# A spectral mixer and a token MLP, forward and backward: one table loaded in two parts, four normal forms on another engine, a first load in two halves, three evictions on another engine

## The chip, the cores and the metric

The kernel runs on one core of one Trainium2 chip. The metric is the device time of one execution in microseconds (us). The core has TensorE (PE, matmuls; its weight loads are PEld), VectorE (DVE), ScalarE (ACT), GpSimd (POOL) and SyncE (SP), which issues most of the DMA transfers. Each engine works through its own instructions in a fixed order and waits on semaphores.

## The reference, cut to what matters

The reference is a forward pass of two blocks and all its gradients but that of B_x:

```python
x = A_x                                   # 1 x 2048 x 448
h  = x + irfft2(rfft2(layernorm(x)) * (w_r + 1j * w_i))
n  = layernorm(layernorm(h))              # one inside block B, one ahead of it
u  = gelu(einsum("bsd,sf->bdf", n, w1) + b1)             # F = 1792
h2 = h + transpose(einsum("bdf,fs->bds", u, w2) + b2)
# and the gradients of h2 for x, w_r, w_i, w1, b1, w2, b2, given grad_out
```

There are eight outputs: h2 and seven gradients. The gradient of w2 (out_6, 1792 x 2048) is gelu's output times grad_out; that of w1 (out_4, 2048 x 1792) is the normalized h times the gradient at gelu's input.

## The kernel before, in words

**Layout.** The 2048 rows are held as 128 partitions of 16 rows each (row 16q + h lies in partition q at place h), so that x, its normal form xln and so on are tiles of 128 x 16 x 448. A group is four of the 16 places.

**Front.** `Norm.stats` takes mean and variance of each place on VectorE (L278, L280). After four places `Norm.finish` (L284) takes the square root on ScalarE, the reciprocal and two small products on VectorE, and then writes the four normal forms. Each is one instruction, either a tensor_scalar on VectorE (L297) or an ACTIVATE on ScalarE (L300); the condition in L296 chooses. `fft_rows` (L304) folds a group into even and odd parts `eo` (L307 to L309, VectorE) and multiplies them by a small table (L315); the four results are evicted into `zt` (L316, through the helper `ev`, whose lines are L194 for ScalarE and L195 for VectorE). All this is run for four groups (L430).

`fft_cols` (L319) then does the column transform: for r = 0, 8 and 1 to 7 it multiplies parts of zt by the table df1 (L333 to L347), evicts (L339 or L350), forms sum and difference on VectorE (`gg`, L353), and calls `out_r` for r and 16 - r, three matmuls with the table `hf` (L325 to L327) and an eviction into xs (L328). hf has three planes: cosines, sines, and the negated sines, which VectorE writes (L462, through `neg`, L198). The first two are loaded by one transfer of 1 MB (L449). `cmul` (L359) multiplies by the spectral weights on VectorE, `ifft_cols` and `ifft_rows` go back. The same functions are run again for the gradient, with the same hf, on zt2 and ds (from L674).

**Loads.** `nxt` (L180) puts each early load behind the one before on SP's queue: x's group 0, half of grad_out (go_nat), x's group 1, the other half of go_nat, the first transposed block of w2 (w2T), x's groups 2 and 3, w2T's next four blocks, the tables df1 and hf, the two halves of w_t, three more blocks of w2T, the other tables. A w2T block needs one of four ring buffers, which `dg` frees.

**Matmuls that fill.** `dg(j)` (L438) needs w2T block j: 16 matmuls of 128 x 448 into one ps_mm buffer, evicted by ScalarE. dg(1) to dg(3) may be issued only after the row transforms of groups 0 to 2, dg(4) and later ones after that of group 3 (L440). `gw2(j)` (L661) computes one block of out_6 as four tiles of 128 x 512, each of four matmuls into a ps_mm buffer and one eviction; the string `on` says by tile which engine evicts. gw2(0) comes ahead of the last row transform, blocks 1 to 13 are written last in the program (L701) with "aaav": ScalarE three times, VectorE once. There are three ps_mm buffers and five ps_sp buffers; the transforms use the latter.

**Order.** The kernel's text isn't the order of the instructions. A planner takes the instruction that is ready and comes first in the text, by prices of its own, engine by engine, before the program is run; that is why dg's and gw2's matmuls lie between those of the transforms. `tc.issue_after(i)` forces what stands under it behind i on i's engine. In the run the order is fixed: an engine waits at an instruction that isn't ready, though later ones may be.

Of the kernel before, what the change touches and what calls it, by code (L numbers as in the profile page):

```python
# [11 lines left out]
BF16 = mybir.dt.bfloat16  # L12
# [5 lines left out]
P = 128  # L18
S = 2048
D = 448  # L20
DF = 225
# [3 lines left out]
NR = 16  # L25
# [4 lines left out]

def _bf(a):
    return np.ascontiguousarray(a.astype(ml_dtypes.bfloat16))


def _tables():

    tb = {}
    q = np.arange(P)
    t_q, pl_q = q // 8, q % 8
    same = (pl_q[:, None] == np.arange(8)[None, :]).astype(np.float64)
    kf = np.zeros((P, 16, 8))
    ke = np.zeros((16, 8, P))
    ko = np.zeros((16, 8, P))
    for r in range(9):
        al = 2 * np.pi * (t_q * r % 16) / 16
        kf[:, r, :] = np.cos(al)[:, None] * same  # L50
        if 0 < r < 8:
            kf[:, 16 - r, :] = -np.sin(al)[:, None] * same
        ke[r] = np.cos(al)[None, :] * same.T
        if 0 < r < 8:
            ke[16 - r] = -np.sin(al)[None, :] * same.T
            ko[16 - r] = -np.sin(al)[None, :] * same.T
        ko[r] = -np.cos(al)[None, :] * same.T
    tb["kf"] = _bf(kf.reshape(P, P))
    tb["kinv"] = _bf(np.stack([ke.reshape(P, P), ko.reshape(P, P), -ko.reshape(P, P)], 1))
    k2 = np.arange(DF)  # L60

    def dtab(scale):
        e = np.zeros((P, 2, DF))
        o = np.zeros((P, 2, 2, DF))
        de = np.stack([np.arange(P), np.arange(P) + 97], 1)
        do = np.stack([np.arange(P) + 1, np.arange(P) + 96], 1)
        for c in range(2):
            e[:, c] = np.cos(2 * np.pi * (de[:, c, None] * k2 % D) / D) * scale
            sn = np.sin(2 * np.pi * (do[:, c, None] * k2 % D) / D) * scale
            o[:, c, 0], o[:, c, 1] = -sn, sn  # L70
        e[: 128 - 97, 1] = 0
        o[: 129 - 96, 1] = 0
        return np.concatenate([e.reshape(P, -1), o.reshape(P, -1)], 1)

    wt = np.full(DF, 2.0 / (S * D))
    wt[[0, DF - 1]] = 1.0 / (S * D)
    tb["df1"] = _bf(dtab(wt))
    tb["df0"] = _bf(dtab(np.ones(DF)))

    def itab(w):  # L80
        a = np.zeros((P, 2, DF))
        b = np.zeros((P, 2, DF))
        d = np.arange(DF)
        for c in range(2):
            kk = np.arange(P) + 97 * c
            th = 2 * np.pi * (kk[:, None] * d[None, :] % D) / D
            a[:, c] = np.cos(th) * w[kk][:, None]
            b[:, c] = np.sin(th) * w[kk][:, None]
        a[: 128 - 97, 1] = 0
        b[: 128 - 97, 1] = 0  # L90
        return np.concatenate([a.reshape(P, -1), b.reshape(P, -1)], 1)

    tb["di0"] = _bf(itab(np.ones(DF)))

    wc = wt.copy()
    wc[0] = 0
    tb["di1"] = _bf(itab(wc))
    pp = np.arange(P)
    p = 16 * (pp % 8) + pp // 8
    r = np.arange(NR)  # L100
    th = 2 * np.pi * (p[:, None, None] * (16 * q[None, None, :] + r[None, :, None]) % S) / S
    tb["hf"] = _bf(np.stack([np.cos(th), np.sin(th)], 1))

    thi = th.transpose(2, 1, 0)
    hi = np.zeros((P, 2, NR, P))
    hi[:, 0, :9], hi[:, 1, :9] = np.cos(thi[:, :9]), np.sin(thi[:, :9])
    hi[:, 0, 9:], hi[:, 1, 9:] = -np.sin(thi[:, 9:]), -np.cos(thi[:, 9:])
    tb["hi"] = _bf(hi)
    tb["ident"] = _bf(np.eye(P))
    return tb  # L110
# [3 lines left out]
def kernel(  # L114
# [21 lines left out]
    ve, ac, po, pe = nc.vector, nc.scalar, nc.gpsimd, nc.tensor  # L136

    consts = ctx.enter_context(tc.tile_pool(name="consts", bufs=1))
# [41 lines left out]
    def nxt(load, *args):  # L180
        if chain:
            with tc.issue_after(chain[-1].ins):
                chain.append(load(*args))
        else:
            chain.append(load(*args))
# [11 lines left out]
    def neg(out, in_):  # L197
        ve.tensor_scalar(out=out, in0=in_, scalar1=-1.0, scalar2=None, op0=ALU.mult)  # L198

    def rows(ap):  # L200
        return ap.rearrange("(q h) d -> q h d", h=NT)


    x = slot(0, [P, NT, D], "x")

    def load_x(g):
        nxt(ld, x[:, 4 * g:4 * g + 4, :], rows(A_x[0])[:, 4 * g:4 * g + 4, :])

    load_x(0)
    tb = _tables()  # L210
    hnd = {k: nc.inline_tensor(v, name=f"tab_{k}") for k, v in tb.items()}
    eps_x = consts.tile([P, 1], F32, name="eps_x")
# [56 lines left out]
    class Norm:  # L269
# [14 lines left out]
        def finish(self, g):  # L284
            mv = self.mv[:, :].rearrange("p (i c) -> p i c", c=2)
            r = self.rstd[:, 4 * g:4 * g + 4]
            sq = col(4, f"sq_{self.nm}")
            ac.activation(out=sq[:], in_=mv[:, :, 1], func=ACT.Sqrt, bias=self.eps_col[:], scale=self.scale)
            ve.reciprocal(out=r, in_=sq[:])
            ve.tensor_scalar(out=self.rneg[:, 4 * g:4 * g + 4], in0=r, scalar1=self.back, scalar2=None, op0=ALU.mult)  # L290
            nb = col(4, f"nb_{self.nm}")
            ve.scalar_tensor_tensor(out=nb[:], in0=mv[:, :, 0], scalar=-1.0, in1=r, op0=ALU.mult, op1=ALU.mult)
            for i in range(4):
                h = 4 * g + i

                if i > 1 and (self.nm == "x" or g == 3):  # L296
                    ve.tensor_scalar(out=self.dst[:, h, :], in0=self.src[:, h, :], scalar1=self.rstd[:, h:h + 1],  # L297
                                     scalar2=nb[:, i:i + 1], op0=ALU.mult, op1=ALU.add)
                else:
                    ac.activation(out=self.dst[:, h, :], in_=self.src[:, h, :], func=ACT.Identity,  # L300
                                  scale=self.rstd[:, h:h + 1], bias=nb[:, i:i + 1])
# [14 lines left out]
            done = ev(zt[:, :, :, 8 * h:8 * h + 8], pz[:, :, :].rearrange("p c (s k) -> p c s k", k=8), on[i])  # L316
        return last, done

    def fft_cols(zt, dtab, dst):  # L319
        e_t = dtab[:, 0:2 * DF].rearrange("p (c k) -> p c k", c=2)  # L320
        o_t = dtab[:, 2 * DF:6 * DF].rearrange("p (c s k) -> p c s k", c=2, s=2)

        def out_r(r, gg):
            px = ps_sp([P, 2 * DF])
            pe.matmul(px[:, :], lhsT=hf[:, 0, r, :], rhs=gg[:, :], start=True, stop=False)  # L325
            pe.matmul(px[:, 0:DF], lhsT=hf[:, 1, r, :], rhs=gg[:, DF:2 * DF], start=False, stop=False)
            pe.matmul(px[:, DF:2 * DF], lhsT=hf[:, 2, r, :], rhs=gg[:, 0:DF], start=False, stop=True)  # L327
            ac.copy(out=dst[:, :, r * DF:(r + 1) * DF], in_=px[:, :].rearrange("p (c k) -> p c k", c=2))  # L328

        for r in (0, 8, 1, 2, 3, 4, 5, 6, 7):  # L330
            pr = ps_sp([P, 2 * DF])
            for c in range(2):
                pe.matmul(pr[:, 0:DF], lhsT=zt[:, c, r, :], rhs=e_t[:, c, :], start=(c == 0), stop=(c == 1))  # L333
            for c in range(2):
                pe.matmul(pr[:, DF:2 * DF], lhsT=zt[:, 2 + c, r, :], rhs=o_t[:, c, 0, :],
                          start=(c == 0), stop=(c == 1))
            if r in (0, 8):
                gg = k1([P, 2 * DF], "gg")
                ac.copy(out=gg[:], in_=pr[:])  # L339
                out_r(r, gg)  # L340
                continue
            pi = ps_sp([P, 2 * DF])
            for c in range(2):
                pe.matmul(pi[:, 0:DF], lhsT=zt[:, 2 + c, 16 - r, :], rhs=o_t[:, c, 1, :],
                          start=(c == 0), stop=(c == 1))
            for c in range(2):
                pe.matmul(pi[:, DF:2 * DF], lhsT=zt[:, c, 16 - r, :], rhs=e_t[:, c, :],  # L347
                          start=(c == 0), stop=(c == 1))
            gi = f2([P, 2 * DF], "gi")
            ac.copy(out=gi[:], in_=pi[:])  # L350
            for rr, op in ((r, ALU.add), (16 - r, ALU.subtract)):
                gg = k1([P, 2 * DF], "gg")
                ve.tensor_tensor(out=gg[:], in0=pr[:], in1=gi[:], op=op)  # L353
                out_r(rr, gg)


    R_GROUPS = ((0, 3), (14, 16), (3, 6), (11, 14), (6, 8), (8, 11))
# [70 lines left out]
    zt = slot(2, [P, 4, NR, P], "zt")  # L428
# [16 lines left out]

    dg(0)
    df1 = table([P, 6 * DF], "df1", "df")
    hf = consts.tile([P, 3, NR, P], BF16, name="hf")
    nxt(ld, hf[:, 0:2], hnd["hf"].ap())  # L449
    w_t = slot(4, [P, 2, XW], "w_t")  # L450
    load_w(w_t, nxt)
    for j in range(1, 4):
# [6 lines left out]
    for g in range(4):  # L459
        nxt(ld, xln_d[:, 4 * g:4 * g + 4, :], xln[:, 4 * g:4 * g + 4, :])  # L460
    with tc.issue_after(folded[3][1].ins):
        neg(hf[:, 2], hf[:, 1])  # L462
    xs = slot(3, [P, 2, XW], "xs")

    def neg_hi(r0, r1, last):
# [1 line left out]
            with tc.issue_after(last.ins):  # L467
                neg(hi[:, 0], hi[:, 2])

    fft_cols(zt, df1, xs)  # L470
    cmul(lambda r0, r1: (w_t[:, 0, r0 * DF:r1 * DF], w_t[:, 1, r0 * DF:r1 * DF]), xs, w_t, False, neg_hi)
    ab = slot(5, [P, 2, 2, NT, NR, 8], "ab")
    ifft_cols(w_t, ab)
# [225 lines left out]
    st(out_7.rearrange("(q h) -> q h", h=NT), gb2b[:])  # L699

    for j in range(1, NFB):  # L701
        s6_st = gw2(j, "aaav")
        if j == 8:
            s6_mid = s6_st

# [69 lines left out]
```

## Time and profile before

| what | us |
|---|---|
| runs: median (lowest to highest of 3) | 370.83 (369.65 to 373.05) |
| the profiled execution | 368.86 |
| its span | 367.1 |
| first matmul starts | 10.43 |
| matmuls, busy | 347.4 |
| VectorE, busy | 236.7 |
| ScalarE, busy | 213.8 |

The span runs from the first to the last instruction that the profile shows; the execution's time has a little more around it. Rows of the timeline are: start in us, length in us, engine, line of the kernel, operation, tile written <- tiles read, shapes, how many were merged into the row, and in brackets how long the engine stood idle ahead of it and what ended that wait. L169 and L175 are the helpers that issue loads and transposing loads, SPq is SP's queue of them: the length of its rows is the time to issue a transfer, not the time until the data is there.

### The profile page before, as it was taken

The numbers are of one execution on the slowest core, as the hardware profiler recorded it, in microseconds if no ns is written. First come the engines' busy times: TensorE is split into PE (matmuls) and PEld (weight loads), VectorE is DVE, ScalarE is ACT, GpSimd is POOL, SyncE is SP. The second block draws the span as 40 slices with busy tenths as digits, with TensorE's granted clock in tenths as the row PEclk, the third lists the DMA queues.
The fourth block names the chain that finished last, engine by engine and source line by source line (L and its number), as shares of the span: only waits on it lengthen the run. The fifth ranks groups of instructions, "written<-read, shape, count | busy, mean of one in ns | idle before, by whom it ended". The sixth has DMA issues, their size and how long they took to land.

```text
span 367.1 us, 5776 instructions
## 1 busy us (share of the span) xinstructions
PE 347.4 (95%) x2115; PEld 200.4 (55%) x2115; DVE 236.7 (64%) x562; ACT 213.8 (58%) x410; POOL 61.3 (17%) x107
## 2 busy tenths in 40 slices
PE   0898999999999999999999999999989999999996
PEld 0555666676655555555555555556655555565553
DVE  4863679887647999422267778378995666698000
ACT  3575554456649996029022245867656676787664
POOL 1000000001122112300630000101012531356211
PEclk9999999999999999999999999999999999999999
DMA  8999999996999999999989793992774444956533
GB/s 286 267 275 292 293 248 271 303 269 223 318 234 217 349 311 349 374 343 205 269 193 186 158 186 159 163 184 96 180 190 186 183 168 162 353 209 241 230 151 150
DMA packets 132524, 86.48 MB, mean 236 GB/s; under 512 B 91952, under 2 KB 123824, under 8 KB 131984
## 3 DMA queue, kind: packets, MB, share of 16 engines
q1 hardware_dynamic: 124304, 55.78, 61.5%
q0 software_dynamic: 8048, 30.31, 22.5%
q8 instruction: 16, 0.26, 0.3%
q14 instruction: 12, 0.10, 0.1%
q10 hardware_dynamic: 144, 0.03, 0.0%
HBM read 32.81 MB, written 30.76 MB: 173 GB/s over the span
## 4 chain that ended last, share of the span: by engine, by line
PE 64%; DVE 20%; ACT 9%; DMA 4%; issue 2%; ACTq 0%; DVEq 0%
PE ps_mm L736 12%; PE ps_mm L666 10%; PE ps_sp L591 7%; PE ps_mm L523 6%; PE ps_sp L523 5%; PE ps_mm L442 5%; PE ps_mm L591 4%; DMA w2T<-in_B_w_dram 3%; DVE junk L619 3%; DVE junk L621 3%; ACT v L614 3%; DVE t_r L366 2%; DVE gg L353 2%; PE ps_sp L415 2%; DVE t_i L367 2%
## 5 line engine op out<-in xcount | busy, mean ns | idle before, releaser
L194 ACT CAST s<-ps_mm 128x512 bf16<-128x512 f32 (+1 forms) x107 | 57.6, 557 | 25.6 <-PE ps_mm L666 11.1
L666 PE MATMUL ps_mm<-goT,g_t 128*128 128x512 bf16 x224 | 55.2, 379 | 1.6 <-ACT s L194 1.5
L442 PE MATMUL ps_mm<-go_nat,w2T 128*128 128x448 bf16 x224 | 50.3, 356 | 1.0 <-DMA w2T<-in_B_w_dram 1.0
L736 PE MATMUL ps_mm<-du_t,hlnT 128*128 128x512 bf16 (+1 forms) x256 | 49.6, 352 | 0.0
L647 PE MATMUL ps_mm<-du,w1T 128*128 128x449 bf16 x224 | 43.4, 353 | 0.0
L736 PEld LDWEIGHTS <-hlnT 128*128 128x128 bf16 x256 | 25.1, 98 | 22.2
L591 PE MATMUL ps_sp<-gT,w2c 128*128 128x448 bf16 x140 | 35.6, 352 | 0.0
L614 ACT ACTIVATE v<-ps_mm,nm,rstd_h 128x448 f32<-128x448 f32 x16 | 11.6, 724 | 40.2 <-DVE nm L612 40.2
L172 POOL DMA_DIRECT2D out_dram<-s x29 | 15.6, 539 | 114.0 <-ACT s L194 87.8
L591 PEld LDWEIGHTS <-w2c 128*128 128x128 bf16 x224 | 21.9, 98 | 20.5
L647 PEld LDWEIGHTS <-w1T 128*128 128x128 bf16 x224 | 21.7, 97 | 20.7
L666 PEld LDWEIGHTS <-g_t 128*128 128x128 bf16 x224 | 21.6, 97 | 20.7 <-issue 1.4
L523 PEld LDWEIGHTS <-w1c 128*128 128x128 bf16 x224 | 21.8, 98 | 20.1 <-issue 1.3
L442 PEld LDWEIGHTS <-w2T 128*128 128x128 bf16 x224 | 21.7, 98 | 16.1 <-DMA w2T<-in_B_w_dram 1.7
L353 DVE TENSOR_TENSOR gg<-ps_sp,gi 128x450 bf16<-128x450 f32 x28 | 16.2, 621 | 17.5 <-ACT gi L350 17.5
L591 PE MATMUL ps_mm<-gT,w2c 128*128 128x448 bf16 x84 | 25.0, 352 | 0.0
L523 PE MATMUL ps_mm<-hln,w1c 128*128 128x448 bf16 x112 | 23.8, 352 | 0.4 <-DVE b1col L512 0.2
L194 ACT CAST eo<-ps_sp 128x450 bf16<-128x450 f32 x32 | 17.2, 538 | 11.0 <-PE ps_sp L415 10.7
L596 DVE SCALAR_TENSOR_TENSOR h<-ps_sp,b2col,hr 128x448 bf16<-128x448 f32 x10 | 6.3, 679 | 25.7 <-PE ps_sp L591 25.7
L523 PE MATMUL ps_sp<-hln,w1c 128*128 128x448 bf16 x112 | 22.6, 352 | 0.0
L619 DVE CUSTOM_DVE_ANT_0 junk<-ps_sp,xr,rneg_x 128x448 bf16<-128x448 f32 x16 | 10.9, 682 | 16.3 <-ACT v L616 16.3
L315 PE MATMUL ps_sp<-kf,eo 128*128 128x128 bf16 x128 | 9.3, 231 | 11.9 <-DVE eo L309 11.9
(148 smaller groups left out, 622.0 us busy)
## 6 DMA issues: line engine op xcount, KB each, us to landing
w1c<-in_B_w_dram SPq DMA_DIRECT2D x7, 1024.0 KB, 8.4
w2c<-in_B_w_dram SPq DMA_DIRECT2D x8, 896.0 KB, 10.8
out_dram<-s POOLq DMA_DIRECT2D x14, 512.0 KB, 3.0
out_dram<-s POOLq DMA_DIRECT2D x15, 448.0 KB, 2.9
xs_d<-xs SPq DMA_DIRECT2D x1, 1800.0 KB, 7.7
xs_b<-xs_d SPq DMA_DIRECT2D x1, 1800.0 KB, 8.1
x<-in_A_x_dram SPq DMA_DIRECT2D x4, 448.0 KB, 4.2
go_nat<-in_grad_out_dram SPq DMA_DIRECT2D x2, 896.0 KB, 6.8
```

The source lines that it names most:

```text
L172: return (eng or po).dma_start(out=out, in_=in_)
L194: return ac.copy(out=out, in_=in_)
L353: ve.tensor_tensor(out=gg[:], in0=pr[:], in1=gi[:], op=op)
L442: pe.matmul(pg[:], lhsT=w2T[j][:, t, :], rhs=go_nat[:, t, :], start=(t == 0), stop=(t == NT - 1))
L523: pe.matmul(pu[:], lhsT=wc[:, h, o:o + P], rhs=hln[:, h, :], start=(h == 0), stop=(h == NT - 1))
L591: pe.matmul(p2[i][:], lhsT=w2c[t0 // 4][:, j, i * P:(i + 1) * P], rhs=gT[:, j, :], start=(j == 0), stop=(j == NFB - 1))
L614: ac.activation(out=v[:], in_=ps[:, 0:D], func=ACT.Identity, scale=rstd_c, bias=nm1[:])
L619: ve.tensor_tensor_reduce(out=junk[:], in0=ps[:, 0:D], in1=xhat, scale=rneg_c, scalar=0.0, op0=ALU.mult, op1=ALU.add, accum_out=nm2[:])
L621: ve.scalar_tensor_tensor(out=junk[:], in0=xhat, scalar=nm2[:], in1=v[:], op0=ALU.mult, op1=ALU.add)
L647: w1_last = pe.matmul(pd[:], lhsT=w1T[:, j, :], rhs=du[:, j, 0:D + 1], start=(j == 0), stop=(j == NFB - 1))
L666: mm = pe.matmul(pw[:], lhsT=g_t[:, c, j * P:(j + 1) * P], rhs=goT[:, c, 512 * n:512 * n + 512], start=(c == 0), stop=(c == 3))
L736: pe.matmul(pw[:, 0:wdt], lhsT=hlnT[:, c, h * P:(h + 1) * P], rhs=du_t[:, c, 512 * n:512 * n + wdt], start=(c == 0), stop=(c == 3))
```

## The change

There are four edits. The table hf is stored and loaded in two parts of eight r each, in the order R_ORDER in which out_r uses them (0, 8, 1, 15, 2, 14, 3, 13, then 4, 12 and so on); the first part is negated where the whole was, the second by a function that fft_cols calls after VectorE's sums for r = 2. In the second use of fft_cols the function isn't given, and the planes are those written in the first. x's group 0 is loaded in two transfers of two places each. The condition for normal forms now puts all four of x's group 3 on VectorE; x's other groups and h's are where they were. gw2's blocks 4, 5 and 6 are evicted by ScalarE alone.

```diff
+R_ORDER = [0, 8] + [k for r in range(1, 8) for k in (r, 16 - r)]
...
@@ -99,7 +102,8 @@
     p = 16 * (pp % 8) + pp // 8
     r = np.arange(NR)
     th = 2 * np.pi * (p[:, None, None] * (16 * q[None, None, :] + r[None, :, None]) % S) / S
-    tb["hf"] = _bf(np.stack([np.cos(th), np.sin(th)], 1))
+
+    tb["hf"] = _bf(np.stack([np.cos(th), np.sin(th)], 1)[:, :, R_ORDER].reshape(P, 2, 2, 8, P).transpose(0, 2, 1, 3, 4))
 
     thi = th.transpose(2, 1, 0)
     hi = np.zeros((P, 2, NR, P))
@@ -206,7 +210,8 @@
     def load_x(g):
         nxt(ld, x[:, 4 * g:4 * g + 4, :], rows(A_x[0])[:, 4 * g:4 * g + 4, :])
 
-    load_x(0)
+    for h in (0, 2):
+        nxt(ld, x[:, h:h + 2, :], rows(A_x[0])[:, h:h + 2, :])
     tb = _tables()
     hnd = {k: nc.inline_tensor(v, name=f"tab_{k}") for k, v in tb.items()}
     eps_x = consts.tile([P, 1], F32, name="eps_x")
@@ -293,7 +298,7 @@
             for i in range(4):
                 h = 4 * g + i
 
-                if i > 1 and (self.nm == "x" or g == 3):
+                if (i > 1 or g == 3) if self.nm == "x" else (i > 1 and g == 3):
                     ve.tensor_scalar(out=self.dst[:, h, :], in0=self.src[:, h, :], scalar1=self.rstd[:, h:h + 1],
                                      scalar2=nb[:, i:i + 1], op0=ALU.mult, op1=ALU.add)
                 else:
@@ -316,15 +321,16 @@
             done = ev(zt[:, :, :, 8 * h:8 * h + 8], pz[:, :, :].rearrange("p c (s k) -> p c s k", k=8), on[i])
         return last, done
 
-    def fft_cols(zt, dtab, dst):
+    def fft_cols(zt, dtab, dst, second=None):
         e_t = dtab[:, 0:2 * DF].rearrange("p (c k) -> p c k", c=2)
         o_t = dtab[:, 2 * DF:6 * DF].rearrange("p (c s k) -> p c s k", c=2, s=2)
 
         def out_r(r, gg):
             px = ps_sp([P, 2 * DF])
-            pe.matmul(px[:, :], lhsT=hf[:, 0, r, :], rhs=gg[:, :], start=True, stop=False)
-            pe.matmul(px[:, 0:DF], lhsT=hf[:, 1, r, :], rhs=gg[:, DF:2 * DF], start=False, stop=False)
-            pe.matmul(px[:, DF:2 * DF], lhsT=hf[:, 2, r, :], rhs=gg[:, 0:DF], start=False, stop=True)
+            k, i = R_ORDER.index(r) // 8, R_ORDER.index(r) % 8
+            pe.matmul(px[:, :], lhsT=hf[:, k, 0, i, :], rhs=gg[:, :], start=True, stop=False)
+            pe.matmul(px[:, 0:DF], lhsT=hf[:, k, 1, i, :], rhs=gg[:, DF:2 * DF], start=False, stop=False)
+            pe.matmul(px[:, DF:2 * DF], lhsT=hf[:, k, 2, i, :], rhs=gg[:, 0:DF], start=False, stop=True)
             ac.copy(out=dst[:, :, r * DF:(r + 1) * DF], in_=px[:, :].rearrange("p (c k) -> p c k", c=2))
 
         for r in (0, 8, 1, 2, 3, 4, 5, 6, 7):
@@ -350,8 +356,10 @@
             ac.copy(out=gi[:], in_=pi[:])
             for rr, op in ((r, ALU.add), (16 - r, ALU.subtract)):
                 gg = k1([P, 2 * DF], "gg")
-                ve.tensor_tensor(out=gg[:], in0=pr[:], in1=gi[:], op=op)
+                last = ve.tensor_tensor(out=gg[:], in0=pr[:], in1=gi[:], op=op)
                 out_r(rr, gg)
+            if r == 2 and second is not None:
+                second(last)
 
 
     R_GROUPS = ((0, 3), (14, 16), (3, 6), (11, 14), (6, 8), (8, 11))
@@ -445,8 +453,9 @@
 
     dg(0)
     df1 = table([P, 6 * DF], "df1", "df")
-    hf = consts.tile([P, 3, NR, P], BF16, name="hf")
-    nxt(ld, hf[:, 0:2], hnd["hf"].ap())
+    hf = consts.tile([P, 2, 3, 8, P], BF16, name="hf")
+    for k in range(2):
+        nxt(ld, hf[:, k, 0:2], hnd["hf"].ap()[:, k])
     w_t = slot(4, [P, 2, XW], "w_t")
     load_w(w_t, nxt)
     for j in range(1, 4):
@@ -459,7 +468,7 @@
     for g in range(4):
         nxt(ld, xln_d[:, 4 * g:4 * g + 4, :], xln[:, 4 * g:4 * g + 4, :])
     with tc.issue_after(folded[3][1].ins):
-        neg(hf[:, 2], hf[:, 1])
+        neg(hf[:, 0, 2], hf[:, 0, 1])
     xs = slot(3, [P, 2, XW], "xs")
 
     def neg_hi(r0, r1, last):
@@ -467,7 +476,12 @@
             with tc.issue_after(last.ins):
                 neg(hi[:, 0], hi[:, 2])
 
-    fft_cols(zt, df1, xs)
+
+    def neg_hf(last):
+        with tc.issue_after(last.ins):
+            neg(hf[:, 1, 2], hf[:, 1, 1])
+
+    fft_cols(zt, df1, xs, neg_hf)
     cmul(lambda r0, r1: (w_t[:, 0, r0 * DF:r1 * DF], w_t[:, 1, r0 * DF:r1 * DF]), xs, w_t, False, neg_hi)
     ab = slot(5, [P, 2, 2, NT, NR, 8], "ab")
     ifft_cols(w_t, ab)
@@ -699,7 +713,7 @@
     st(out_7.rearrange("(q h) -> q h", h=NT), gb2b[:])
 
     for j in range(1, NFB):
-        s6_st = gw2(j, "aaav")
+        s6_st = gw2(j, "aaaa" if 4 <= j <= 6 else "aaav")
         if j == 8:
             s6_mid = s6_st
```

## The prediction

> **What bounds the kernel now.** I read the busy table first, then TensorE's own rows in order of time, looking only for the spots where it stands, then the rows of the engine or queue named there as releaser.
>
> ```profile
> span 367.1 us, 5776 instructions
> PE 347.4 (95%) x2115; PEld 200.4 (55%) x2115; DVE 236.7 (64%) x562; ACT 213.8 (58%) x410; POOL 61.3 (17%) x107
> ```
>
> TensorE (PE) works 95% of the span. It starts at 10.43 us, and from there to its last matmul it hardly stands still, because low-priority matmuls (dg, then gelu_in, gw2, the last product) are put into every hole. A change can only win by an earlier useful start or by removing one of the few stands. These are the stands that this change can touch, and the row that causes each:
>
> ```profile
> 10.43 1.89 PE L315 MATMUL ps_sp<-kf,eo 128*128 128x128 bf16 x16 [10.43 <-DVE eo L309]
> 16.59 1.07 PE L315 MATMUL ps_sp<-kf,eo 128*128 128x128 bf16 x16 [0.55 <-DVE eo L309]
> 23.14 1.07 PE L315 MATMUL ps_sp<-kf,eo 128*128 128x128 bf16 x16 [0.38 <-DVE eo L309]
> 28.16 1.07 PE L315 MATMUL ps_sp<-kf,eo 128*128 128x128 bf16 x16 [0.35 <-DVE eo L309]
> 36.24 0.55 PE L442 MATMUL ps_mm<-go_nat,w2T 128*128 128x448 bf16 x2 [0.98 <-DMA w2T<-in_B_w_dram]
> ```
>
> The first four are the row transform of x's four groups, each waiting for VectorE's eo. The fifth is dg(5), waiting for its transposed block of w2. Why the fourth is late, and when hf was usable:
>
> ```profile
> 23.46 0.70 DVE L297 TENSOR_SCALAR xln<-x,rstd_x,nb_x 128x448 bf16<-128x448 bf16 x2
> 24.12 2.03 ACT L194 CAST zt<-ps_sp 128x512 bf16<-128x512 f32 x4
> 26.02 0.79 ACT L300 ACTIVATE xln<-x,nb_x,rstd_x 128x448 bf16<-128x448 bf16 x1
> 26.84 0.63 DVE L307 TENSOR_TENSOR eo<-xln 128x892 bf16<-128x892 bf16 x1 [2.68 <-ACT xln L300]
> 30.02 0.68 DVE L198 TENSOR_SCALAR hf<-hf 128x2048 bf16<-128x2048 bf16 x1
> ```
>
> One of group 3's four normal forms sits behind four evictions on ScalarE, and VectorE idles 2.68 us for it. The negation of hf (30.02) starts when hf lands: issued at 22.90, 6.9 us to landing, so 29.8.
>
> ```profile
> 10.40:36.20 25.80, 23.55 (x166) 14.07 (x166) 16.42 (x52) 16.85 (x33) 0.00 (x0) 1.00 1.06 280
> 24.48 9.60 SPq L175 DMA_TRANSPOSE w2T<-in_B_w_dram  x1
> ```
>
> The first row (a stretch; busy of PE, PEld, DVE, ACT, POOL, then granted clock, DMA share, GB/s) says that the DMA engines are full, share 1.06, from the start to 36 us. The second is the transfer dg(5) waits for: its issue ends at 34.08 and it lands at 36.2, 2.1 later (the first w2T block likewise: issue ends 10.17, landed 12.29). Faster compute doesn't bring it sooner.
>
> The gw2 stage:
>
> ```profile
> 272.89 0.59 ACT L194 CAST s<-ps_mm 128x512 bf16<-128x512 f32 x1 [0.49 <-PE ps_mm L666]
> 273.52 0.81 PE L666 MATMUL ps_mm<-goT,g_t 128*128 128x512 bf16 x3 [0.67 <-ACT s L194]
> 274.56 1.29 DVE L195 CAST s<-ps_mm 128x512 bf16<-128x512 f32 x2
> 275.42 0.38 PE L666 MATMUL ps_mm<-goT,g_t 128*128 128x512 bf16 x1 [0.67 <-ACT s L194]
> ```
>
> Counting L666 matmuls from 233.1 (16 to a block; some records may be missing) puts block 4 at about 252 to 260, block 5 at 260 to 271, block 6 at 272 to 277. Their VectorE evictions (n = 3) come only at 274.56 (two of them) and 278.52, as VectorE is busy 13.85 of 14.00 us from 262 to 276. Two of the three ps_mm buffers are held meanwhile, and PE stands twice, 0.67 each, for ScalarE to free the third.
>
> **The change part by part.**
>
> *x's first group in two loads.* One more SP issue (0.39 to 0.57 in the rows) ahead of go_nat, x's group 1, go_nat's second half and the first w2T block. That block's issue lasts 7.37 us because data, not SP, is behind, so the issue is covered; without that cover it costs 0.45 on all that follows. The first half is 229 KB ahead of the second; at the 382 GB/s of 4 to 6 us that is 0.6, so statistics begin 0.6 earlier (bounds 0, if both land together, and 0.9), and group 0's matmuls start at about 9.8. PE gains none of it there: dg(0) waits for its w2T block at 12.29 either way, 0.24 after the last weight load of L315. What is left is VectorE's lead at group 1: its eo comes 0.3 to 0.6 earlier, so the 0.55 stand shrinks. Then dg(1) needs the second w2T block, whose issue ends at 15.25, so about 17.35, where PE is at 17.5 now. I carry 0.3 of lead on.
>
> *Normal forms.* Only x's group 3 changes (h's condition comes to what it was): two 0.75 us ACTIVATEs leave ScalarE, two 0.35 us operations join VectorE, which idles there. All four are done at 23.46 + 4 x 0.35 = 24.86, so eo starts 1.98 earlier than 26.84, the fourth L315 at 26.2, and fft_cols' first L333 at about 28.2 in place of 30.2 (27.9 with the lead).
>
> *hf in two.* One more SP issue (0.43) ahead of w_t and the sixth w2T block, covered as SP runs ahead of the data there too (9.60 us for one block's issue). The first half lands half of 1 MB sooner: 524 KB at the 415 to 425 GB/s of 26 to 32 us is 1.25, so 28.55. Its negation is half of 0.68 plus a little, 0.4: done at 28.95. It is first needed by L327 of r = 0, now 1.46 after the first L333, so at 29.4 to 29.7: no wait, 0.45 to spare. With one transfer it would be done at 30.5 and take back about one of the two microseconds, so these two parts belong together. The second negation (0.4) follows the r = 2 sums on VectorE, with its half landed at 29.8 and the first use at r = 4; behind it wait cmul and the next sums, VectorE is busy 0.94 of 4.00 us from 36 to 40: nothing. The two halves cost 0.1 more VectorE time in all.
>
> *What this buys on PE.* Until dg(5)'s block lands, PE has only the row transforms, dg(0) to dg(4) and the pieces of fft_cols. From the third L315 on it has 38 filler matmuls (6, 13, 3, 16 by the rows), and before the change they run out one row pair into fft_cols. With group 3 at 26.2, some ten are used ahead of it instead of 19, and the rest lasts one row pair longer: out of r = 1 and 15 (3 matmuls each, 0.77 in all) and the first products of r = 2 (0.77). PE reaches dg(5) at about 35.9 with 1.5 us more work behind it and waits for the same 36.2. So the front gives 1.5, not the 2 to 2.6 by which its steps move. Bounds: 0, if the order puts dg(5) where it is now (then PE waits longer for the same landing), and 2.6, all the stands above after 12 us plus some of the start.
>
> *gw2's blocks 4 to 6.* Three 0.65 us evictions leave VectorE, three of 0.59 join ScalarE, which is busy 9.80 of 14.00 us from 248 to 262 and 7.60 of 14.00 from 262 to 276: room for all three. The buffers come free about 1 us after their last matmul instead of 14, so both stands go: 1.34 by the rows, 1.66 if the 0.16 by which a matmul's row outlasts its slot is counted in each. I take 1.5; bounds 0 (ScalarE late in its turn) and 2.2 (the smaller holes of 262 to 272 too). ScalarE's gi and ds copies may now stand behind an eviction, 0.59 each; PE has gw2 as filler to 310, so that costs nothing unless the filler itself is what waits. Next late there is ab on VectorE, unchanged, ending at about 274.
>
> After both places PE is full to the end (33.87 of 34.00 from 276 to 310, 23.67 of 24.00 from 340 to 364) and then follow one eviction and one store, as now. So what is gained stays gained.
>
> **Sum.** The profiled execution took 368.86 (span 367.1 and 1.76 around it). 368.86 - 1.5 - 1.5 = 365.9. It lies 1.97 under the median of the three runs shown, 370.83; on that scale the forecast is 370.83 - 3.0 = 367.8, 0.8% less. A measurement of this kernel tells about 1% (3.7 us) from no change, so "no change that shows" is likeliest.
>
> **The rivals.**
> - Front absorbed: dg(5) keeps its place in PE's fixed order, the 0.98 stand grows, only gw2's 1.5 is left: 369.3. For it: the order already put dg(5) ahead of the sums once, 1 us before the block was there. Against: filler is taken when nothing else is ready, and more is ready. 0.2.
> - gw2's part hidden: the two stands stay because ScalarE's own order delays the evictions; 1.5 from the front alone, 369.3. For it: both stands name ScalarE. Against: the two buffers held by VectorE. 0.12.
> - More: every stand up to 36 us and gw2's 2.2 go, 370.83 - 2.6 - 2.2 = 366.0. 0.14.
> - Slower, by the order: the instruction order is made anew. In fft_cols seven to nine filler matmuls stand between a pair's products and its sums, 1.3 to 1.7 us against 0.2 + 0.54 (gi) + 0.03 + 0.64 (gg) = 1.4 plus. If the new order puts two fewer there, each of the 14 places (two tables) stands 0.38 longer: 5.3 against the gains of 3.0, 373.1. It decides from 1.1 matmuls a place. For it: 0.15 is lost at two places already. 0.12.
> - Slower, by DMA: if each of the two added transfers held the one queue for the 2.1 us between issue end and landing, dg(5)'s block would land at 40.4, costing 4.2, less gw2's 1.5 and the 1.5 pulled forward: 372.0; even from 39.2 on. Against it: w_t's two loads, issued 0.48 apart, land 8.6 and 10.4 after issue, 2.3 apart, and 922 KB in that is 400 GB/s with no such gap. 0.05.
>
> The Trainium skill, Perfetto Trace Analysis, section DMA Optimizations, says that small DMAs under 2 KB carry a significant overhead each; x's rows go from 3,584 to 1,792 bytes a partition, so by that rule this last rival gets weight, and the sum would be its 372.0 at worst. This trace shows no 1,792-byte load to test it on.
>
> **How the numbers follow.** My forecast (both gains, 2.2 to 3.8) has 0.37; the rivals 0.2, 0.12, 0.14, 0.12, 0.05. Faster by over 1% are the "more" case and half of the forecast's: 0.32. Slower by over 1% (374.5) takes three matmuls a place in the order rival, or disturbed early loads: 0.1. Within 1%: 0.58. The range leaves out the far half of "more" and the far part of both slower ones: 364.8 to 371.8.
>
> **What would show it.** Right: eo of group 3 at about 24.6; the first L333 near 28; the negation of hf near 28.6 and two of them; dg(5)'s first matmul still near 36.2, but after the outputs of r = 1; no L195 s row between 262 and 277 and no stand of PE there. Wrong: w2T landing after 37; stands of 0.3 or more at each L325; the stands at 273 and 275 still there.

## The result, and the profile after

The changed kernel takes 369.01 us (median of 22 runs, 367.92 to 371.32), the kernel before, on the same chip, 370.10 (22 runs, 369.32 to 373.05). The ratio is 0.996, with a 95% interval from 0.9944 to 0.9976: 1.5 us or 0.4% faster, inside the 1% that the prediction called no change. (The ratios here are worked out from all runs of both kernels; the two medians differ by 1.1 us.) The forecast was 367.8, a gain of 3.0, so half of the expected gain or less came. The two halves of the sum didn't come alike: the back gained more than was forecast, the front nothing that shows.

The span and the busy times of the changed kernel:

```profile
span 366.2 us, 5763 instructions
PE 346.6 (95%) x2100; PEld 200.7 (55%) x2115; DVE 236.3 (65%) x562; ACT 213.2 (58%) x411; POOL 61.2 (17%) x107
```

Nothing is to be seen there: the same 95% of TensorE, the same busy times. The rows of the timeline tell it. First the front of the changed kernel, of three engines and SP's queue, in order of time (helpers' and kernel's lines are a few higher than before: L320 was L315, L339 was L333, L450 was L442). Before, three of these rows were:

```profile
2.80 7.37 SPq L175 DMA_TRANSPOSE w2T<-in_B_w_dram  x1
12.30 3.75 PE L442 MATMUL ps_mm<-go_nat,w2T 128*128 128x448 bf16 x15
231.96 1.07 PE L315 MATMUL ps_sp<-kf,eo 128*128 128x128 bf16 x16 [0.21 <-DVE eo L309]
```

After:

```profile
2.76 1.01 SPq L173 DMA_DIRECT2D go_nat<-in_grad_out_dram  x1
3.81 8.69 SPq L179 DMA_TRANSPOSE w2T<-in_B_w_dram  x1
9.71 1.89 PE L320 MATMUL ps_sp<-kf,eo 128*128 128x128 bf16 x16 [9.71 <-DVE eo L314]
14.61 3.92 PE L450 MATMUL ps_mm<-go_nat,w2T 128*128 128x448 bf16 x12 [3.02 <-DMA w2T<-in_B_w_dram]
25.76 1.32 DVE L302 TENSOR_SCALAR xln<-x,rstd_x,nb_x 128x448 bf16<-128x448 bf16 x4
27.18 0.63 DVE L312 TENSOR_TENSOR eo<-xln 128x892 bf16<-128x892 bf16 x1
28.50 1.07 PE L320 MATMUL ps_sp<-kf,eo 128*128 128x128 bf16 x16 [0.45 <-DVE eo L314]
31.32 0.43 DVE L202 TENSOR_SCALAR hf<-hf 128x1024 bf16<-128x1024 bf16 x1 [0.87 <-DMA hf<-tab_hf]
32.05 0.36 PE L339 MATMUL ps_sp<-df,zt 128*128 128x225 bf16 x2
39.50 1.50 PE L450 MATMUL ps_mm<-go_nat,w2T 128*128 128x448 bf16 x7
233.23 1.07 PE L320 MATMUL ps_sp<-kf,eo 128*128 128x128 bf16 x16 [0.21 <-DVE eo L314]
```

The first matmul starts 0.72 earlier (9.71 for 10.43), and all four normal forms stand on VectorE in one row. But the issue of the first transposed block of w2 begins 1.0 later than before and lasts 8.69 for 7.37, and TensorE stands 3.02 for that block: it is there at 14.61, not by 12.30. From there on the front is late: group 3's eo starts at 27.18 (before 26.84), fft_cols at 32.05 (30.21), dg(5) at 39.50 (36.24). Before dg(5) one more row pair is done, worth 1.54, so dg(5) is 1.7 late at equal work. The last row is a good mark for all that follows: it is the second half of the row transform of the last group in the backward pass, the last place where TensorE waits for anything ahead of gw2's blocks 4 to 6. It was at 231.96 before. So in these two executions the front has lost 1.27.

What the DMA engines did while that block was held up, before (first fence) and after (second); the columns are those of the prediction's stretch, the last two the DMA share and the GB/s:

```profile
4.00:6.00 2.00, 0.00 (x0) 0.00 (x0) 1.72 (x5) 0.00 (x0) 0.00 (x0) 1.00 1.10 382
```

```profile
4.00:6.00 2.00, 0.00 (x0) 0.00 (x0) 2.00 (x8) 0.00 (x0) 0.00 (x0) 1.00 0.74 184
```

Half of the rate is gone for two microseconds, when x's first two places have landed (statistics start at 3.55 and go on to the other two without a wait) and, by the order of the issues, go_nat and x's next group are on their way.

Now gw2's stage after the change. The stands at 273.52 and 275.42 are gone, VectorE's late s rows too, and ScalarE takes the evictions in turn:

```profile
273.13 2.11 PE L680 MATMUL ps_mm<-goT,g_t 128*128 128x512 bf16 x9
273.98 0.58 ACT L198 CAST s<-ps_mm 128x512 bf16<-128x512 f32 x1 [0.39 <-PE ps_mm L680]
274.85 0.58 ACT L198 CAST s<-ps_mm 128x512 bf16<-128x512 f32 x1 [0.28 <-PE ps_mm L680]
275.27 1.24 PE L680 MATMUL ps_mm<-goT,g_t 128*128 128x512 bf16 x5
276.55 0.81 PE L680 MATMUL ps_mm<-goT,g_t 128*128 128x512 bf16 x3
```

From the mark to the end of the span it was 367.1 - 231.96 = 135.14, now it is 366.2 - 233.23 = 132.97: this part has gained 2.17. Front and back together are the 0.9 between the two spans.

### The profile page after: what moved, and what is told of

The parts are those of the page before. It is cut to its first block, busy times and chain, and to the rows that moved or that the text cites. A ratio compares the mean times of both kernels' runs of the same rounds, so it can differ in the third digit from the quotient of the medians.

```text
span 366.2 us, 5763 instructions
## 1 busy us (share of the span) xinstructions
PE 346.6 (95%) x2100; PEld 200.7 (55%) x2115; DVE 236.3 (65%) x562; ACT 213.2 (58%) x411; POOL 61.2 (17%) x107
## 4 chain that ended last, share of the span: by engine, by line
PE 63%; DVE 17%; ACT 6%; DMA 5%; issue 5%; SPq 2%; POOL 1%; ACTq 0%; POOLq 0%; DVEq 0%
PE ps_mm L750 12%; PE ps_mm L680 10%; PE ps_mm L450 6%; PE ps_mm L537 6%; PE ps_sp L605 6%; PE ps_sp L537 5%; DMA w2T<-in_B_w_dram 3%; PE ps_mm L605 3%; DVE junk L633 3%; DVE junk L635 3%; ACT v L628 3%; PE ps_sp L423 2%; DVE t_r L374 2%; PE ps_sp L421 2%; DVE gg L359 2%
## 5 line engine op out<-in xcount | busy, mean ns | idle before, releaser
L198 ACT CAST s<-ps_mm 128x512 bf16<-128x512 f32 x110 | 59.5, 558 | 23.8 <-PE ps_mm L680 8.1
L680 PE MATMUL ps_mm<-goT,g_t 128*128 128x512 bf16 x214 | 53.0, 379 | 0.6 <-ACT s L198 0.2
L450 PE MATMUL ps_mm<-go_nat,w2T 128*128 128x448 bf16 x224 | 50.5, 361 | 3.1 <-DMA w2T<-in_B_w_dram 3.0
L450 PEld LDWEIGHTS <-w2T 128*128 128x128 bf16 x224 | 21.9, 99 | 19.0 <-DMA w2T<-in_B_w_dram 4.1
L320 PE MATMUL ps_sp<-kf,eo 128*128 128x128 bf16 x128 | 9.3, 231 | 10.7 <-DVE eo L314 10.7
```

What stands on the lines that cost most here:

```text
L198: return ac.copy(out=out, in_=in_)
L450: pe.matmul(pg[:], lhsT=w2T[j][:, t, :], rhs=go_nat[:, t, :], start=(t == 0), stop=(t == NT - 1))
L680: mm = pe.matmul(pw[:], lhsT=g_t[:, c, j * P:(j + 1) * P], rhs=goT[:, c, 512 * n:512 * n + 512], start=(c == 0), stop=(c == 3))
```

## The experiments

The theory at this point: gw2's edit gives about two microseconds; earlier normal forms would give one or two more, but each transfer added to SP's queue, which is full from the start, makes all w2T blocks behind it later, and TensorE, which runs in a fixed order, then stands for them. The rivals: the new order of the instructions takes the gain of the front away whenever the blocks land; the small rows of the added transfers are what costs, not their number; the cut of hf matters only together with w_t's loads, or only when the normal forms are earlier. Where the texts on record use letters, C is "the arrival of the blocks binds, whatever the order on the queue", E is "the number of transfers on SP's queue, not the size of their rows", and G is "hf's cut costs only together with the earlier normal forms".

The first four take the change apart.

**e1_no_x**: the change with x's group 0 in one load.

```diff
-    for h in (0, 2):
-        nxt(ld, x[:, h:h + 2, :], rows(A_x[0])[:, h:h + 2, :])
+    load_x(0)
```

> The changed kernel with x's group 0 in one load again (three edits left). Theory A: cutting that load in two slows the one queue of early loads, so that the first transposed w2 block lands at 14.6 us in place of 12.3 and dg(5)'s at about 38.9 in place of 36.2; this takes back what the front would gain. Then without the cut the first block lands at 12.3 again, dg(5) starts at 36.2 to 36.5 with one more row pair done, and the kernel gains the front's 1.5 and gw2's 2.2: about 3.7 us, ratio 0.990. Theory B: the late block is an accident of the profiled execution and the front gives nothing anyway, because dg(5) waits for its block in either order: ratio 0.996, as the whole change.

Measured: 368.55 against 370.55, ratio 0.9934 (0.9908 to 0.9959). Its rows at TensorE's stands, and group 3's way (eo started at 24.92):

```profile
29.59 0.36 PE L338 MATMUL ps_sp<-df,zt 128*128 128x225 bf16 x2
30.37 0.43 DVE L202 TENSOR_SCALAR hf<-hf 128x1024 bf16<-128x1024 bf16 x1 [2.20 <-DMA hf<-tab_hf]
38.02 1.50 PE L449 MATMUL ps_mm<-go_nat,w2T 128*128 128x448 bf16 x7 [1.09 <-DMA w2T<-in_B_w_dram]
57.19 0.55 PE L449 MATMUL ps_mm<-go_nat,w2T 128*128 128x448 bf16 x2 [1.25 <-DMA w2T<-in_B_w_dram]
77.39 0.74 PE L449 MATMUL ps_mm<-go_nat,w2T 128*128 128x448 bf16 x3 [0.91 <-DMA w2T<-in_B_w_dram]
```

Without x's cut the 3.02 at the first block is gone, and three stands have come at later blocks, two of them where the kernel before had none. So x's cut isn't all of the loss.

**e2_x_only**: the kernel before with x's cut alone.

```diff
-    load_x(0)
+    for h in (0, 2):
+        nxt(ld, x[:, h:h + 2, :], rows(A_x[0])[:, h:h + 2, :])
```

> The kernel before with x's group 0 in two loads, nothing else. Theory A: the first matmul comes at 9.7 in place of 10.4, but the first w2 block lands near 14.6 and dg(0) starts there; slower by 1.5 to 2.5 us, ratio 1.004 to 1.007. Theory B: the block lands at 12.3 to 12.7, ratio 0.999 to 1.000.

Measured: 371.84 against 370.55, ratio 1.0041 (1.0019 to 1.0062): slower by itself. The row of its first w2T block and the stretch from 4 to 6 us are those of the whole change:

```profile
14.47 3.90 PE L443 MATMUL ps_mm<-go_nat,w2T 128*128 128x448 bf16 x12 [2.83 <-DMA w2T<-in_B_w_dram]
```

```profile
4.00:6.00 2.00, 0.00 (x0) 0.00 (x0) 2.00 (x8) 0.00 (x0) 0.00 (x0) 1.00 0.77 203
```

**e3_gw2_only**: the kernel before with gw2's edit alone.

```diff
-        s6_st = gw2(j, "aaav")
+        s6_st = gw2(j, "aaaa" if 4 <= j <= 6 else "aaav")
```

> The kernel before with blocks 4 to 6 of gw2 evicted by ScalarE alone. Theory A (the whole gain of the change comes from here and is larger than forecast): TensorE's two stands near 273 and 275 us and the small holes about them go, 2.2 us, ratio 0.994. Theory B: 1.5 us, ratio 0.996, and the change's other parts add up to nothing.

Measured: 367.91 against 370.55, ratio 0.9929 (0.9901 to 0.9956), 2.6 us. By the ratios one line gains more by itself than the four edits together (0.996), though the two intervals overlap by 0.0012. In the profile the stretch from the mark to the end is 133.19 for 135.14, so 1.95 comes from there.

**e4_norm_hf**: normal forms and hf's cut, without the other two (e1 with gw2 as before).

> The kernel before with hf in two parts and all four of x's last normal forms on VectorE, x's first load and gw2 as before. Theory A: fft_cols starts 2 us earlier, dg(5)'s block still lands at 36.2, and one more row pair lies ahead of it: 1.5 us faster, ratio 0.996. Theory B: the wait for the block grows by what was gained: within 0.3 us, ratio 0.999 to 1.001.

Measured: 370.35 against 370.55, ratio 0.9986 (0.9958 to 1.0014): nothing. It has e1's stands (at 38.08, 57.56 and 77.88).

The next four ask what it is in a transfer.

**e5_x_parts**: the kernel before, x's group 0 in two transfers of 64 partitions each, so that the rows keep their 3,584 bytes.

```diff
-    load_x(0)
+    for q in (0, 64):
+        nxt(ld, x[q:q + 64, 0:4, :], rows(A_x[0])[q:q + 64, 0:4, :])
```

> The kernel before, with x's group 0 in two loads cut by partitions (0 to 63 and 64 to 127), so that there is one transfer more, as in the change, but its rows stay 3,584 bytes. Theory A1, the row size: rows of 1,792 bytes upset the loads behind them; here go_nat starts at its full rate of 350 to 380 GB/s, the first w2 block lands at 12.3 to 12.6, time as before (ratio 0.999 to 1.001). Theory A2, one transfer more on the queue: go_nat starts at 110 to 270 GB/s as with the other cut, the block lands near 14.5, ratio 1.003 to 1.006.

Measured: 371.92 against 369.81, ratio 1.0059 (1.0037 to 1.0081). Slower, with rows of the old size. But this cut does something else as well: x's group 0 itself lands later (statistics start at 5.37, before at 4.28), so the first matmul starts at 11.53, and TensorE then hardly stands for the first w2T block (its row starts at 13.55).

**e6_x_act**: the kernel before, x's group 0 cut by places as in the change (rows of 1,792 bytes), the second half on ScalarE's queue.

```diff
-    load_x(0)
+    nxt(ld, x[:, 0:2, :], rows(A_x[0])[:, 0:2, :])
+    ld(x[:, 2:4, :], rows(A_x[0])[:, 2:4, :], ac)
```

> The kernel before, with x's group 0 cut as in the change (rows of 1,792 bytes), but the second half issued by ScalarE's queue, behind kf. SP's queue holds as many transfers as before, and go_nat follows the first half at 1.2 us. A1, row size: go_nat slow, block near 14.5, ratio 1.003 to 1.006. A2, number of transfers on SP's queue: go_nat at full rate, block at 12.3 to 12.7, ratio 0.999 to 1.001.

Measured: 369.59 against 369.81, ratio 0.9998 (0.9972 to 1.0025). The stretch from 4 to 6 us of e5 (first) and e6 (second):

```profile
4.00:6.00 2.00, 0.00 (x0) 0.00 (x0) 0.63 (x2) 0.00 (x0) 0.00 (x0) 1.00 1.01 310
```

```profile
4.00:6.00 2.00, 0.00 (x0) 0.00 (x0) 1.71 (x5) 0.00 (x0) 0.00 (x0) 1.00 1.10 370
```

With small rows on the other queue the rate is nearly that of the kernel before (382), and the first w2T block's issue ends at 10.31 (before 10.17, in the change 12.50). With large rows in two transfers on SP's queue it ends at 11.40. So rows of 1,792 bytes aren't the cause by themselves: the added transfer costs on SP's queue (e2) and not on ScalarE's (e6). That large rows cost the same way isn't shown, since e5 loses its time, as far as its rows tell, at x itself; and as the dip is 310 there and 184 to 203 with small rows on SP's queue, their size may add to it. Nothing was won in e6 either: its first matmul started at 10.45, no earlier than before.

**e7_w2T_first**: e1 with the sixth w2T block ahead of w_t's two loads.

```diff
-    load_w(w_t, nxt)
-    for j in range(1, 4):
+    dg(1)
+    load_w(w_t, nxt)
+    for j in range(2, 4):
         dg(j)
```

> The three edits without the cut of x (normal forms, hf in two, gw2), and in addition the two loads of w_t put behind the sixth w2 block in the queue. Theory C: the front is bound by the arrival of w2's blocks, so what the earlier fft_cols wins is waited away at blocks 5, 8 and 11 (stands of 1.25, 1.40 and 1.07 us). Then dg(5)'s block lands some 4 us earlier, its stand goes, but the stands at blocks 8 and 11 stay or grow, as the queue carries the same bytes: 0 to 1.2 us faster than without the move, ratio to the kernel before 0.990 to 0.9935. Rival D: the stands are a matter of that one block's place in the queue, and all of the 3 us goes: 0.985.

Measured: 367.73 against 369.81, ratio 0.9956 (0.9932 to 0.998); e1 had 0.9934, so no gain shows. In the profiled execution the stand at the sixth block is gone, and a larger one has come three blocks on:

```profile
58.20 0.55 PE L449 MATMUL ps_mm<-go_nat,w2T 128*128 128x448 bf16 x2 [3.09 <-DMA w2T<-in_B_w_dram]
```

Another place in the queue moves the wait, it doesn't take it away: this fits C, that the blocks' arrival as a whole binds. It gives no support to the rival that hf's cut costs only next to w_t's loads, since those now stand behind a block.

**e8_norm_gw2**: the change without either cut, so with no transfer added.

```diff
-                if i > 1 and (self.nm == "x" or g == 3):
+                if (i > 1 or g == 3) if self.nm == "x" else (i > 1 and g == 3):
...
-        s6_st = gw2(j, "aaav")
+        s6_st = gw2(j, "aaaa" if 4 <= j <= 6 else "aaav")
```

> The kernel before with the normal forms and gw2's evictions of the change; hf and x in one load each. If hf in two parts is needed to use the earlier normal forms, hf's negation (landing at 29.8 to 30.4, 0.7 us) holds up the first outputs and the kernel is 0.5 to 1.5 us slower than with both: ratio 0.995 to 0.998. If hf in two brings nothing because its first half lands no sooner (30.36 in two runs), it is the same as with both or faster: ratio 0.991 to 0.9935.

Measured: 366.06 against 369.81, ratio 0.9893 (0.9865 to 0.9922): 4.0 us, well apart from the change's interval. Its rows:

```profile
26.54 1.07 PE L315 MATMUL ps_sp<-kf,eo 128*128 128x128 bf16 x16 [0.28 <-DVE eo L309]
29.90 0.36 PE L333 MATMUL ps_sp<-df,zt 128*128 128x225 bf16 x2
31.07 0.69 DVE L198 TENSOR_SCALAR hf<-hf 128x2048 bf16<-128x2048 bf16 x1 [2.59 <-DMA hf<-tab_hf]
```

VectorE waits 2.59 for the uncut hf, which the cut was to spare (with the cut it waited 2.20 in e1), and TensorE's weight loads wait 0.3 for it. The prediction had it that one hf transfer "would be done at 30.5 and take back about one of the two microseconds, so these two parts belong together". It was done at 31.76, and the times show nothing taken back: e8 has 0.9893, e1 with the cut 0.9934. The rival that the new order alone takes the gain away finds no support here either.

The last four ask about hf.

**e9_hf_one**: e1 with hf in its two-part order, but in one transfer; both negations as in the change.

```diff
-    for k in range(2):
-        nxt(ld, hf[:, k, 0:2], hnd["hf"].ap()[:, k])
+    nxt(ld, hf[:, :, 0:2], hnd["hf"].ap())
```

> The change without the cut of x, and hf in its two-part layout loaded by one transfer (rows of 4,096 bytes, two to a partition), still negated in two parts. Theory E: what hurts is the number of transfers on SP's queue, as for x. Then this is as fast as normal forms and gw2's edit with hf whole, or up to 0.4 us faster for the shorter first negation: ratio 0.988 to 0.9895. Theory F: the smaller rows or the new layout hurt: 0.993, as with two transfers.

Measured: 366.57 against 370.48, ratio 0.9879 (0.9843 to 0.9916). One transfer fewer than e1 is worth 2 us by the ratios; the intervals overlap by a little (e1's begins at 0.9908). The waits of TensorE's matmuls for w2T in the first 100 us (total, times, longest) in e1 and in e9:

```profile
PE ps_mm L449 <- DMA w2T<-in_B_w_dram: 3.2, 3, 1.2
```

```profile
PE ps_mm L449 <- DMA w2T<-in_B_w_dram: 1.0, 2, 0.7
```

And SP's rows of the sixth to eighth block, three issues in each row, again e1 and e9; the last issue ends at 41.02 and at 39.46:

```profile
27.71 13.31 SPq L179 DMA_TRANSPOSE w2T<-in_B_w_dram  x3
```

```profile
24.91 14.55 SPq L179 DMA_TRANSPOSE w2T<-in_B_w_dram  x3
```

**e10_hf_only**: the kernel before with hf's cut alone (e4 with the old condition for normal forms).

> The kernel before with hf in two transfers and two negations, nothing else. Theory E: the later w2 blocks come later (the third after hf ends its issue about 1.4 us after its time before) and TensorE waits for them at dg: 0.5 to 1.5 us slower, ratio 1.001 to 1.004. Rival G: the cut costs only together with the earlier normal forms, which make TensorE reach dg's blocks sooner: 0.999 to 1.001.

Measured: 370.71 against 370.48, ratio 1.0003 (0.9976 to 1.003): by the times no cost. The profiled execution, 0.96 above the median of its kernel, shows the stand all the same:

```profile
38.02 0.55 PE L449 MATMUL ps_mm<-go_nat,w2T 128*128 128x448 bf16 x2 [2.44 <-DMA w2T<-in_B_w_dram]
```

**e11_hf_act**: normal forms, gw2 and hf's cut, the second half of hf on ScalarE's queue, behind its evictions of group 1; x in one load.

```diff
-    for k in range(2):
-        nxt(ld, hf[:, k, 0:2], hnd["hf"].ap()[:, k])
+    nxt(ld, hf[:, 0, 0:2], hnd["hf"].ap()[:, 0])
...
+    with tc.issue_after(folded[1][1].ins):
+        ld(hf[:, 1, 0:2], hnd["hf"].ap()[:, 1], ac)
```

> Normal forms, gw2's edit and hf in two transfers, the second half issued by ScalarE's queue behind its evictions of group 1; x in one load. Theory E: SP's queue holds as many transfers as before the change, so the cost of the cut goes, and the first half of hf lands about 1 us sooner than the whole: ratio 0.986 to 0.9895. Theory F, or contention of the two queues: 0.992 to 0.994.

Measured: 366.99 against 370.48, ratio 0.9879 (0.9845 to 0.9912). The same two transfers as in e1, of the same size, one of them on another queue: the loss doesn't show (e1's interval and this one overlap by 0.0004).

**e12_hf_x**: the whole change, but hf in one transfer as in e9.

> The whole change, but hf's two parts loaded by one transfer. If the costs of the two cuts add up (x's 1.5 us, hf's 1.5 us), this lies between the change (0.996) and the version with neither cut (0.989): 0.9915 to 0.993. If one cut hides the other, since dg(5)'s block is late already with x cut: 0.9955 to 0.997.

Measured: 369.84 against 370.48, ratio 0.9979 (0.995 to 1.0008). So x's cut takes 3.7 us on top of e9 (0.9879 to 0.9979, intervals apart). With x cut, taking hf's second transfer away gives nothing back that shows (0.996 for the whole change): the two costs don't add.

All kernels by two measures. The third column is the end of SP's row for the sixth to eighth block, the fourth is the mark, the last group's second row of kf,eo, the fifth the span less the mark. The last column is the front by the times: (ratio - 1) x 370.2, plus the 1.9 of the back where gw2's edit is in.

| kernel | edits | eighth block issued | mark | mark to end | ratio | front, by times |
|---|---|---|---|---|---|---|
| before | none | 38.56 | 231.96 | 135.14 | 1 | 0 |
| after | norm, x, hf, gw2 | 41.24 | 233.23 | 132.97 | 0.996 | +0.4 |
| e1 | norm, hf, gw2 | 41.02 | 233.73 | 132.97 | 0.9934 | -0.5 |
| e2 | x | 42.62 | 235.10 | 135.00 | 1.0041 | +1.5 |
| e3 | gw2 | 38.92 | 232.81 | 133.19 | 0.9929 | -0.7 |
| e4 | norm, hf | 41.18 | 234.21 | 134.89 | 0.9986 | -0.5 |
| e5 | x by partitions | 40.23 | 233.01 | 135.09 | 1.0059 | +2.2 |
| e6 | x, other queue | 39.30 | 235.13 | 134.87 | 0.9998 | -0.1 |
| e8 | norm, gw2 | 39.66 | 231.33 | 133.07 | 0.9893 | -2.1 |
| e9 | norm, gw2, hf order | 39.46 | 231.51 | 133.09 | 0.9879 | -2.6 |
| e10 | hf | 40.76 | 235.02 | 134.88 | 1.0003 | +0.1 |
| e11 | norm, gw2, hf on two queues | 39.17 | 230.90 | 134.30 | 0.9879 | -2.6 |
| e12 | norm, x, hf order, gw2 | 43.13 | 234.65 | 133.05 | 0.9979 | +1.1 |

(e7 loads in another order; its mark is 235.74, its back 132.96. With its own back, which gained 0.84, e11's last column would be -3.6.) Three things are to be read here. The third column parts the kernels: where a transfer was added to SP's queue, the eighth block is issued at 40.23 or later (seven kernels), in all others at 39.66 or earlier (six, with e6 and e11, which put the added transfer on ScalarE's queue). How many were added doesn't order them: e2 with one has 42.62, the change with two 41.24. The fifth column is the same within 0.3 for all kernels without gw2's edit and within 0.25 for those with it, e11 aside, which has a stand of 1.02 of its own at 282.86: the back is settled by one profile. The mark isn't: before and e3 have the same front and lie 0.85 apart, and a profiled execution lies up to 2.8 above (e7) and 2.1 below (e5) the median of its own kernel. Executions differ in the front, where the loads run, so the front is judged by the times of many runs, and the profile only says by what wait it is lost. How far the times tell it apart is shown by e3, whose front is that of the kernel before and which has -0.7 in the last column.

Of two marks a part is TensorE's granted clock. In e6 TensorE stood 2.30 for the sixth block (to 37.57), and behind that the clock was 0.50 from 38 to 41 us; in e7 it stood 3.09 (to 58.20), and the clock was 0.50 from 60 to 62. By the mean clock of the stretches about them (0.76 and 0.67 from 36 to 42 in e6, 0.86 and 0.58 from 57 to 63 in e7) this is 1.7 us each, an estimate. It doesn't follow each long stand: behind 2.44 in e10, 2.83 in e2 and 3.02 in the change the granted clock stayed at 1.00.

## Why the prediction was right and wrong

The time was inside the range, and the forecast erred by 1.2 us. In part that is luck. The forecast set out from 370.83, the median of three runs, where 22 runs give 370.10; as a gain it was 3.0, and 1.1 by the medians or 1.5 by the ratio came. And of its two terms one was too small (gw2) and the other didn't come: by the times the front stands at +0.4 us (-0.2 to +1.0), where a gain of 1.5 was forecast.

**x in two loads: the step that failed.** The step said: "That block's issue lasts 7.37 us because data, not SP, is behind, so the issue is covered". What was said of x itself held (group 0's matmuls at 9.71, forecast 9.8). But the added transfer wasn't covered. The first w2T block came at 14.61 in place of 12.3, 2.3 late, not the 0.45 of one issue that the step gave as its price without cover, and e2 shows this with nothing else changed. By the times x's cut costs 1.5 us alone and 3.7 on top of e9. The mechanism is that of the rival to which the prediction gave 0.05, a price of 2.1 for each transfer added, "dg(5)'s block would land at 40.4"; dg(5) started at 39.50. The argument against that rival was drawn from w_t's two loads, which follow one another without a gap. They are plain loads; the case to be priced was a transposing load behind an added plain one, and no row bounded it from above. That the queue was behind should have been read the other way: here every kernel with a transfer added to it had the eighth block later than before, by 1.6 us or more (third column), and TensorE stands as soon as it comes to a block ahead of its landing, as it did at 36.24 before. Of the signs of being wrong that the prediction named, "w2T landing after 37" came (39.50).

The Trainium skill, Perfetto Trace Analysis, section DMA Optimizations, says that splitting a transfer may help if the DMA engines are generally idle. The trace agrees from the other side: their share was 1.10 from 4 to 6 us before, and the split made the kernel slower (e2). The same section of the Trainium skill puts a significant overhead on DMAs under 2 KB, which the prediction had weighed for this rival. It speaks of whole transfers, and these are of 229 KB; the prediction read it as a rule for their rows. By the runs small rows alone aren't what decides: with rows of 1,792 bytes and the second half on ScalarE's queue nothing is lost (e6, 0.9998).

**Normal forms.** Where nothing else is late, the step was right: eo of group 3 at 24.92 in e1, forecast 24.86. In the change it is at 27.18, as x's later groups are issued behind the late first block (12.55). The next step, "fft_cols' first L333 at about 28.2", was wrong even so: 29.59 in e1, 29.90 in e8. Ahead of group 3, 11 matmuls of filler were used in the change (forecast ten), and 14 were put between group 3's row transform and fft_cols, where there had been six. That lost little, as filler is work that has to be done. By the times the front with the earlier normal forms and without a burden on the queue gains 2.1 (e8) to 2.6 (e9); the forecast had 1.5. From e3 to e8, the cleanest comparison of normal forms alone, it is 0.9929 to 0.9893, 1.3 us, and the intervals overlap: their own share isn't settled. e9 and e11 (0.9879) lie below e3 too, with intervals that overlap its own.

**hf in two.** The first half was to land at 28.55. It was used at 30.37 in e1 and 31.32 in the change, later than the whole had been (30.02). It didn't make fft_cols wait in the change, since that began later still. The step's "covered as SP runs ahead of the data there too" failed as x's did: from e9 to e1 the second transfer costs 2 us by the ratios, and e1's profile has stands at three w2T blocks. The intervals of e8, e9 and e11 all overlap e1's a little (by 0.0004 to 0.0014), so this cost is likely, not shown as x's is. That it costs nothing in e10 fits G: without earlier normal forms TensorE comes to the blocks later and has slack; but e10's interval reaches to +0.3%, and its profile has a stand of 2.44, so this is not settled.

**dg(5) waits for the same 36.2.** Half right: one row pair more was done ahead of it. Its landing moved with the queue.

**gw2.** Right in place and mechanism: the buffers held by VectorE's late evictions were the cause, both stands are gone, and in the change and e3 nothing came back behind (in e11 a stand of 1.02 did, for VectorE's next eviction). The size was off: forecast 1.5, measured 1.95 (e3) and 2.17 (the change) from mark to end, and 2.6 by e3's times, whose interval (1.6 to 3.7) holds them. The ten microseconds from 40 behind the mark, which held the two stands, have 8.62 us of matmuls before and 9.92 after, 1.3 of it; the rest is spread and no row names it. "What is gained stays gained" held.

The rival "front absorbed" (369.3) comes nearest by its number, the rival "slower, by DMA" by its mechanism: the front's gain was paid out for transfers, for x's by e2 and e12, for hf's by ratios whose intervals overlap. The best versions are e9 and e11 (0.9879) and e8 (0.9893), which are not told apart: each beats the kernel before and the change, and e8 does it with two of the four edits.

## What to carry to other kernels

Price an added transfer at what it does to the transfers behind it on its queue, not at its issue time; where the queue is full and a fixed order of matmuls waits for its blocks, put it on another queue or leave it out. Take a change with several edits apart, for one good edit can hide a bad one: here one line by itself was worth as much as the whole, or more. And look for evictions that hold buffers on a busy engine: two stands of 0.67 were worth two microseconds.

## What the runs showed of the hardware

An added transfer on SP's queue delayed a transposing load behind it by 2.3 us, five times the 0.45 of an issue, and the rate fell to 184 GB/s at a share of 0.74 meanwhile; with the second half on ScalarE's queue it was 370. Why go_nat's second half is slow to start behind the added transfer isn't settled: the views of the trace give each queue's packets only as totals. An added transfer for which nothing is cut was not tried.

A mean share over a long stretch hides holes. The kernel before, at a mean share of 1.06 up to 36 us, has this microsecond about the end of w_t's loads (they land at 32.0 and 34.2 by the prediction's figures), where the sixth block's transposing load is next:

```profile
33.00:34.00 1.00, 1.00 (x11) 0.90 (x10) 0.00 (x0) 0.43 (x1) 0.00 (x0) 1.00 0.39 28
```

It moved 28 GB/s, where the stretch had 280. This hole in front of the very block that TensorE stood for at 36.24 was not seen when the prediction called the DMA engines full. It isn't of this execution alone: in e9, 31 GB/s were moved from 34 to 35 us. Its cause is open, and whether it can be filled was not tried.
